# Block-sparse attention with a top-k expert: one-block steps of two batches rewritten as two-block units of one batch

## The chip, the cores and the metric

The kernel runs on one core of one Trainium2 chip. The metric is the device time of one execution in microseconds (us), taken as the median of several runs. The core has five engines with a program each: TensorE (PE) multiplies matrices into PSUM, VectorE (DVE), ScalarE (ACT) and GpSimd (POOL) work on tiles of 128 partitions, and SyncE (SP) issues DMA transfers. In the profile PEld is TensorE's weight load. GpSimd also issues DMA transfers whose rows are given by an index tile (gathers); they run on queue 0, SyncE's on queue 1, and both on the same 16 DMA engines.

## The reference

The inputs are q, k and v of 4 batches, 8 heads, 768 positions and 64 values per head, in float32. Positions fall into 24 blocks of 32. A query block sees the blocks beside it, itself, blocks 0 and 23, and three sampled blocks; query blocks 0 and 23 see everything.

```python
mask = np.abs(blk_i - blk_j) <= 1
mask = mask | (blk_i == 0) | (blk_j == 0) | (blk_i == 23) | (blk_j == 23)
for qb in range(24):
    for kb in sampled_blocks[qb]:
        mask[qb * 32:(qb + 1) * 32, kb * 32:(kb + 1) * 32] = True
attn = softmax(np.where(mask, q @ k.T / 8, -1e9))      # per batch and head
x = (attn @ v), heads side by side                      # [4, 768, 512]
scores = x @ w_gate                                     # [4, 768]
for b in range(4):                                      # the 128 best tokens of a batch
    top = argpartition(-scores[b], 128)[:128]
    ye = np.maximum(x[b, top] @ w1, 0) @ w2             # 512 -> 1024 -> 512
    out[b, top] = x[b, top] + sigmoid(scores[b, top])[:, None] * ye
```

## The kernel before

The work is a list of 60 tasks. 44 of them are interior tasks (`"i", h, i`): query block i (1 to 22) of the two batches 2h and 2h+1, all 16 heads. The other 16 are global tasks (`"g", b, c`): query blocks 0 and 23 of batch b against all 768 keys, for the two heads of pair c.

An interior task works as follows. `int_keys` lays eight key blocks for both batches side by side in a ring buffer `kg`: blocks 23, i-1, i, i+1 and the three sampled ones and block 0. VectorE copies the window of one batch, GpSimd that of the other (L295), and ScalarE the six sampled blocks, whose offsets it loads into registers. `int_values` loads the values of the window (`vw`, 96 rows of 4,160 bytes) over SyncE and gathers the sampled rows (`vr`) with GpSimd (L310). `int_scores` runs 32 matmuls of 64x32 weights over 256 key columns (L67 by way of `mm`), `int_softmax` takes the maxima and scales them, `int_exp` makes four exponentials, `int_transpose` turns the result in eight 128x128 pieces and evicts it on ScalarE and VectorE (which multiplies by `keep` to drop repeated blocks), and `int_out` runs 64 matmuls of 128x32 weights over 65 columns, normalises, stores the rows and adds up the gate's scores.

The tasks overlap by steps: in step s the scores of task s, the transposes of task s-1, the exponentials of task s and the output of task s-2 are issued. TensorE, VectorE, ScalarE and the loads keep the order in which they are written.

The routing (`route`) of a batch spreads the 768 scores over all partitions, builds comparison masks on VectorE (`p4`), counts them with matmuls on TensorE (`p5`), turns the ranks into a selection, and gathers the 128 chosen rows from the output. The expert splits every float32 operand into two float32r parts, so that a product is three. `expert(0, ...)` serves batches 0 and 1, `expert(2, ...)` batches 2 and 3; both run when the last attention tasks are ending or done, in an order written out by hand at the bottom of the function. In it, products with 256 and 512 columns alternate with the routing of batches 2 and 3.

Of the kernel before, what the change touches and what calls it, by code (L numbers as in the profile page):

```python
# [1 line left out]

# [15 lines left out]
PSUM = bass.MemoryType.PSUM  # L18

# [3 lines left out]
NPAIR = H // 2  # L23
VW = H * (D + 1)
# [4 lines left out]
NRING = 3  # L29
NKG = 3  # L30
WARM = 26
AHEAD = 1
SCALE = 0.125


@with_exitstack
def block_sparse_attention_moe(ctx, tc, qg, qi, kt, v1, blocks, w_gate, w1, w2, outs):
# [4 lines left out]
    inp = ctx.enter_context(tc.tile_pool(name="inp", bufs=3))  # L42
    ring = ctx.enter_context(tc.tile_pool(name="ring", bufs=1))
    work = ctx.enter_context(tc.tile_pool(name="work", bufs=3))
# [3 lines left out]
    ps_s = ctx.enter_context(tc.tile_pool(name="ps_s", bufs=2, space=PSUM))  # L48
# [4 lines left out]
    blk32 = blocks.bitcast(I32)  # L53
    flat = blk32.rearrange("(o a) b -> o (a b)", o=1)

    loads, pe, copied = [], [], []
    filled = set()
    inorder = [True]

    def queue(i):  # L60
        if inorder[0]:
            if pe:
                tc.add_manual_dep(i.ins, pe[-1].name, NOSYNC, reason="PE in order")
            pe.append(i.ins)

    def mm(*args, **kw):
        queue(nc.tensor.matmul(*args, **kw))  # L67

    def trans(*args, **kw):
        queue(nc.tensor.transpose(*args, **kw))  # L70


    class Pinned:
        """An engine whose instructions keep the order in which they are written."""

        def __init__(self, engine):
            self.engine, self.on, self.last = engine, True, None

        def __getattr__(self, name):
            def call(*args, **kw):  # L80
                i = getattr(self.engine, name)(*args, **kw)  # L81
                if self.on:
                    if self.last is not None:
                        tc.add_manual_dep(i.ins, self.last.name, NOSYNC, reason="in order")
                    self.last = i.ins
                return i
            return call

    vec, act = Pinned(nc.vector), Pinned(nc.scalar)

    def load(dst, src):
        i = nc.sync.dma_start(dst, src)  # L92
        if loads:
            tc.add_manual_dep(i.ins, loads[-1].name, NOSYNC, reason="loads in order")
        loads.append(i.ins)

# [1 line left out]
    def load_k(b, n):  # L98
        k_sb = ks[b] = inp.tile([P, NPAIR, NB, BLK], F32, tag="k", name=f"k{b}")
        c = NB // n  # L100
        return [lambda p=p, t=t: load(k_sb[:, p, t * c:(t + 1) * c], kt[b, :, p, t * c:(t + 1) * c])
                for p in range(NPAIR) for t in range(n)]

    def load_v(b):
        v_sb = vs[b] = inp.tile([P, S // P, VW], F32, tag="v", name=f"v{b}", bufs=1)
        src = v1[b // 2 * S:(b // 2 + 1) * S, (b % 2) * VW:(b % 2 + 1) * VW]
        if b == 0:
            c = 2 * (D + 1)
            return [lambda p=p: load(v_sb[:, :, p * c:(p + 1) * c],
                                     src[:, p * c:(p + 1) * c].rearrange("(t r) c -> r t c", r=P))  # L110
                    for p in range(NPAIR)]
        return [lambda t=t: load(v_sb[:, t], src[t * P:(t + 1) * P]) for t in range(S // P)]

    def load_qg(b):
        q_sb = inp.tile([P, NPAIR, P], F32, tag="qg", name=f"qg{b}", bufs=2)
        if b == 0:
            load(q_sb[:, 0], qg[b, :, 0])
            return q_sb
        load(q_sb, qg[b])
        return q_sb  # L120

    rb_i = const.tile([P, NB, 3, 2], I32, name="rb_i")
    qgs, qs, ks, vs = {}, {}, {}, {}
    qgs[0] = load_qg(0)
    lk, lv = load_k(0, 1), load_v(0)
    for t in range(2):
        load(ks[0][:, 0, 12 * t:12 * t + 12], kt[0, :, 0, 12 * t:12 * t + 12])
    load(rb_i.rearrange("p a b c -> p (a b c)"), flat.broadcast_to([P, NB * 6]))
    load(qgs[0][:, 1:], qg[0, :, 1:])
    lk[1]()  # L130
    for f in (lk[2], lv[0], lk[3], lv[1]):
        f()

# [4 lines left out]
    for t in range(WARM):  # L138
        nc.tensor.matmul(pw[:, 0:P], none, none, start=True, stop=True)
# [3 lines left out]
    nc.gpsimd.memset(ones, 1.0)  # L143
    warm = const.tile([P, 1], F32, name="warm")
    act.activation(warm, ones[:, 0:1], AF.Exp)
    upper = const.tile([P, P], F32, name="upper")
    nc.gpsimd.affine_select(upper, ones, pattern=[[1, P]], compare_op=ALU.is_gt, fill=0.0,
                            base=0, channel_multiplier=-1)
    one = const.tile([P, 1], BF16, name="one")
    vec.memset(one, 1.0)  # L150
    slot = const.tile([P, P], BF16, name="slot")
    nc.gpsimd.iota(slot, pattern=[[1, P]], base=0, channel_multiplier=0,
                   allow_small_or_imprecise_dtypes=True)
    # token of column c of the score row: blocks 0 and 23 come first
    tok = const.tile([P, S // P], F32, name="tok")
    nc.gpsimd.iota(tok, pattern=[[P, S // P]], base=-BLK, channel_multiplier=1,
                   allow_small_or_imprecise_dtypes=True)
    nc.gpsimd.iota(tok[0:BLK, 0:1], pattern=[[0, 1]], base=0, channel_multiplier=1,
                   allow_small_or_imprecise_dtypes=True)
    nc.gpsimd.iota(tok[BLK:2 * BLK, 0:1], pattern=[[0, 1]], base=S - BLK, channel_multiplier=1,  # L160
                   allow_small_or_imprecise_dtypes=True)

# [1 line left out]
    rb = const.tile([P, NB, 3], F32, name="rb")  # L164
    koff = const.tile([1, NB, 4], I32, name="koff")
    p32 = const.tile([P, 1], F32, name="p32")
    idx_f = const.tile([P, NB], F32, name="idx_f")
    idx = const.tile([P, 2, NB], U32, name="idx")
# [3 lines left out]
    dif = const.tile([P, NB, 3], F32, name="dif")  # L172
    keep = const.tile([P, NB], F32, name="keep")
    keep_w = const.tile([P, 1], F32, name="keep_w")
    d32 = const.tile([P, BLK], F32, name="d32")
    d64 = const.tile([P, 2 * BLK], F32, name="d64")
    tokb = const.tile([P, S // P, 2], BF16, name="tokb")

    # iden[p, q] summed over head quadrants: delta(p % 32, q) and delta(p % 64, q)
    vec.tensor_reduce(d32, ident.rearrange("p (h q) -> p q h", h=4), AX.X, ALU.add)  # L180
    vec.tensor_reduce(d64, ident.rearrange("p (h q) -> p q h", h=2), AX.X, ALU.add)
    # a token as two bf16 values that add to it
    vec.tensor_copy(tokb[:, :, 0], tok)
    vec.tensor_tensor(tokb[:, :, 1], tok, tokb[:, :, 0], ALU.subtract)
    # of the sampled blocks: their offsets in a row of keys, rows to gather
# [10 lines left out]
    for h in range(2):  # L196
        nc.gpsimd.tensor_scalar_add(idx[:, h], idx_f, float(h * S))
# [604 lines left out]
```

## Time and profile before

| | before |
|---|---|
| median of 3 runs | 362.99 us (362.63 to 365.73) |
| span of the profiled execution, first to last instruction | 362.1 us |
| busy: TensorE, VectorE, ScalarE, GpSimd | 282.0, 249.0, 198.9, 124.6 us |
| DMA | 71.20 MB, 197 GB/s over the span |

The page gives the profiled execution's span and no other time of it; the median of the runs is 0.9 us above that span. Times in the trace count from the start of the span. A row of a stretch (A:B) gives its length and then each engine's busy time with the number of its instructions, the granted TensorE clock as a share of full speed, the mean busy share of the DMA engines (which can exceed 1.0 by a little) and what they moved.

### The profile page before, as it was taken

The page shows a single profiled execution, that of the slowest core. Times are in us where ns is not written, and L with a number is a line of the kernel's source. Part 1 is how long each engine was busy: PE and PEld are TensorE (multiplying, and loading weights), DVE is VectorE, ACT ScalarE, POOL GpSimd, SP SyncE. Part 2 cuts the span into 40 slices and gives each one's busy share as a digit, 9 for nine tenths or more (in the row PEclk, how much of TensorE's full clock was granted, in tenths as well). Part 3 has the DMA queues.
Part 4 walks back from the last instruction along what each step waited for, and adds up shares of the span by engine and source line. Part 5 has one row for each costly group of instructions (what it writes and reads, how often), then busy time and mean ns, then how long its engine had stood idle before and what let it go on. Part 6 is the DMA issues. An engine that isn't in the chain of part 4 may idle for free.

```text
span 362.1 us, 14408 instructions
## 1 busy us (share of the span) xinstructions
PE 282.0 (78%) x5706; PEld 208.5 (58%) x5706; DVE 249.0 (69%) x792; ACT 198.9 (55%) x627; POOL 124.6 (34%) x192
## 2 busy tenths in 40 slices
PE   6972938395668978987667799775969999999992
PEld 4552725263446656664434576444657678878982
DVE  2772847656657997897499989987778976972010
ACT  2681729466747885485656468774657762321310
POOL 4850316444433421243453404322212312424421
PEclk9988776978986999999698999988789999999997
DMA  6999799988997997699999737799877510011000
GB/s 203 360 219 225 213 275 267 254 264 231 286 239 228 250 272 242 220 249 271 270 256 228 218 100 198 204 264 249 238 233 208 162 53 23 17 31 58 31 29 29
DMA packets 45162, 71.20 MB, mean 197 GB/s; under 512 B 6953, under 2 KB 29225, under 8 KB 45097
## 3 DMA queue, kind: packets, MB, share of 16 engines
q1 hardware_dynamic: 39529, 50.63, 50.8%
q0 software_dynamic: 5568, 19.67, 19.4%
q8 instruction: 45, 0.74, 0.9%
q14 instruction: 20, 0.16, 0.2%
HBM read 62.93 MB, written 7.35 MB: 194 GB/s over the span
## 4 chain that ended last, share of the span: by engine, by line
DMA 47%; PE 16%; DVE 14%; issue 9%; SPq 6%; POOL 3%; ACT 2%; POOLq 0%; ACTq 0%; DVEq 0%
DMA out<-x 11%; DMA vw<-v 11%; DMA v<-v 7%; DMA w<-w 7%; DMA q<-qi 5%; PE o L67 4%; SPq L92 4%; DVE c L81 3%; PE gs L67 3%; DVE mx L81 3%; PE pt L70 2%; SPq L379 2%; DMA k<-kt 2%; DMA sb<-row 2%; PE s L67 2%
## 5 line engine op out<-in xcount | busy, mean ns | idle before, releaser
L67 PE MATMUL o<-vw,tw 128*32 128x65 f32 x1408 | 51.4, 239 | 41.0 <-DMA vw<-v 27.6
L81 ACT ACTIVATE pr<-s,mx 128x256 f32<-128x256 f32 x176 | 69.2, 480 | 17.2 <-DVE mx L81 17.0
L310 POOL DMA_INDIRECT vr<-v,idx x44 | 42.6, 968 | 86.7 <-PE o L67 80.2
L67 PE MATMUL s<-kg,q 64*32 64x256 f32 x1408 | 57.8, 434 | 15.0 <-ACT kg L81 10.0
L67 PEld LDWEIGHTS o<-vw,tw 128*32 128x32 f32 x1408 | 38.1, 120 | 50.6 <-issue 48.3
L70 PE MATMUL pt<-ident,pr 128*128 128x128 f32 x352 | 61.3, 313 | 6.7 <-ACT kg L81 2.9
L70 PEld LDWEIGHTS pt<-ident,pr 128*128 128x128 f32 x352 | 44.7, 157 | 34.0 <-ACT pr L81 18.5
L81 DVE TENSOR_SCALAR tr<-pt,keep 128x256 f32<-128x256 f32 x88 | 40.0, 479 | 31.5 <-ACT tw L81 30.2
L81 ACT COPY kg<-k 128x128 f32 x264 | 57.5, 313 | 3.5 <-issue 2.9
L81 DVE TENSOR_REDUCE mx<-s 128x4 f32<-128x1024 f32 x44 | 53.5, 1217 | 2.2 <-PE s L67 2.1
L67 PE MATMUL o<-vr,tr 128*32 128x65 f32 x1408 | 51.2, 238 | 3.5 <-issue 3.5
L81 ACT COPY tw<-pt 128x256 f32<-128x256 f32 x84 | 30.5, 380 | 40.8 <-PE o L67 33.6
L295 POOL COPY kg<-k 128x384 f32<-128x384 f32 x44 | 23.3, 531 | 57.5 <-PE s L67 34.5
L67 PEld LDWEIGHTS o<-vr,tr 128*32 128x32 f32 x1408 | 39.6, 121 | 4.2 <-issue 4.1
L67 PEld LDWEIGHTS s<-kg,q 64*32 64x32 f32 x1408 | 23.9, 116 | 29.1 <-ACT kg L81 10.3
L81 DVE TENSOR_TENSOR x<-o,z 128x256 f32<-128x256 f32 x44 | 18.7, 424 | 20.1 <-DMA out<-x 18.4
L257 POOL TENSOR_TENSOR w_l<-w,w_h 128x512 fp32r<-128x512 f32 x16 | 21.3, 1333 | 24.6 <-ACT w_h L81 23.3
L81 DVE CUSTOM_DVE_ANT_0 j<-x,wg_i 128x128 f32<-128x128 f32 x88 | 26.3, 298 | 3.0
L67 PE MATMUL gs<-k,qg 128*128 128x384 f32 x64 | 25.7, 526 | 1.7 <-DMA k<-kt 1.7
L81 ACT CAST w_h<-w 128x512 fp32r<-128x512 f32 x16 | 10.0, 625 | 26.1 <-DMA w<-w 25.0
L81 DVE TENSOR_SCALAR c<-sb,sc 128x128 bf16<-128x128 f32 (+5 forms) x44 | 23.0, 562 | 0.1
L81 DVE COPY kg<-k 128x384 f32<-128x384 f32 (+1 forms) x68 | 22.4, 360 | 0.2 <-DMA k<-kt 0.2
(118 smaller groups left out, 396.2 us busy)
## 6 DMA issues: line engine op xcount, KB each, us to landing
vw<-v SPq DMA_DIRECT2D x44, 390.0 KB
q<-qi SPq DMA_DIRECT2D x44, 128.0 KB
out<-x SPq DMA_DIRECT2D x88, 64.0 KB
v<-v SPq DMA_DIRECT2D x18, 260.0 KB
k<-kt SPq DMA_DIRECT2D x11, 384.0 KB
w<-w SPq DMA_DIRECT2D x16, 256.0 KB
v<-v SPq DMA_DIRECT2D x4, 390.0 KB
k<-kt SPq DMA_DIRECT2D x12, 128.0 KB
```

What stands on the lines that cost most here:

```text
L67: queue(nc.tensor.matmul(*args, **kw))
L70: queue(nc.tensor.transpose(*args, **kw))
L81: i = getattr(self.engine, name)(*args, **kw)
L92: i = nc.sync.dma_start(dst, src)
L257: nc.gpsimd.tensor_tensor(wl, f, wh, ALU.subtract)
L295: copied.append(nc.gpsimd.tensor_copy(kgt[:, 1, :, 1:4], ks[2 * h + 1][:, :, i - 1:i + 2]).ins)
L310: nc.gpsimd.indirect_dma_start(out=vr[n][0:3 * BLK], out_offset=None, in_=v1[:, :], in_offset=bass.IndirectOffsetOnAxis(ap=idx[0:3 * BLK, ...
L379: nc.sync.dma_start(outs[b][i * BLK:(i + 1) * BLK].rearrange("q (p c) -> p q c", p=NPAIR), xe)
```

## The change

The kernel is written anew around the unit (`b, u`): the two query blocks 2u-1 and 2u of one batch, eight heads, 44 units in all. Four key blocks are shared by both query blocks (0, 23, 2u-1, 2u); each query block has four own ones besides: three sampled and the remaining neighbour. A repeated sampled block is replaced by the keys of another slot and an all-zero value row (a 25th block of zeros is added to the values), so no mask is multiplied.

- Shared keys are read in place by the score matmul; own keys are copied to `kr`, four sampled ones and the neighbours by GpSimd with offsets from registers (four loaded per unit), two sampled ones by ScalarE.
- Values of the own blocks are gathered by GpSimd (two gathers of 128 rows of 2,080 bytes per unit, into four buffers); those of the shared blocks are loaded by SyncE (64 rows per unit; blocks 0 and 23 once per buffer and batch, five buffers).
- Queries are scaled by 1/8 on VectorE before use, so maxima and exponentials need no scale.
- The global query blocks are two steps per batch, each for four heads.
- The 52 steps are laid out with fixed slots: in step s the transposes and output of step s, the exponentials of s+1, the scores and maxima of s+2 and the gather of s+3 are issued, and every engine, SyncE and GpSimd among them, keeps the written order.
- Weights are loaded and split in steps 1 to 18, the low part on VectorE (before: GpSimd).
- A batch's routing and expert are spread over 28 steps that begin after its last unit: ranks are counted on VectorE by comparisons that accumulate, and the expert runs on one batch with 512-column products. Batch 3 spreads its scores with a matmul instead of by way of DRAM.
- The area kept for GpSimd's DMA descriptors is set to 8,192 bytes per partition.

```diff
+    def load_vs(b, u):
+        i = vs_of(b, u)
+        r = rows_of(b, 2 * u - 1)
+        sp.dma_start(vss[i][0:64], vt[r:r + 64])
+        if vs_b[i] != b:
+            vs_b[i] = b
+            for n, j in enumerate((0, NB - 1)):
+                r = rows_of(b, j)
+                sp.dma_start(vss[i][64 + 32 * n:96 + 32 * n], vt[r:r + BLK])
...
+    def w_split(i):
+        if i in stage:
+            wh, wl, f = ws[i][0], ws[i][1], stage.pop(i)
+            act.copy(wh, f)
+            vec.tensor_tensor(wl, f, wh, ALU.subtract)
...
+    def gather(b, u):
+        kr = krs[b, u] = inp.tile([P, 2, NP, KW], F32, tag="kr", name=f"kr{b}_{u}", bufs=3)
+        vr = vrs[b, u] = inp.tile([P, 2, VR], F32, tag="vr", name=f"vr{b}_{u}", bufs=4)
+        for e in range(2):
+            pool.indirect_dma_start(
+                out=vr[:, e], out_offset=None, in_=vt[:, :],
+                in_offset=bass.IndirectOffsetOnAxis(ap=vidx[:, b, u - 1, e:e + 1], axis=0))
+        flat = ks[b].rearrange("p j c -> p (j c)")
+        o = offs.pop((b, u, POOL))
+        for e in range(2):
+            for s in range(2):
+                pool.tensor_copy(kr[:, e, s], flat[:, ds(o[2 * e + s], KW)])
+        w = [slot_of(2 * u - 2), slot_of(2 * u + 1) if u < NU - 1 else slot_of(0)]
+        pool.tensor_copy(kr[:, :, 3], ...)
...
+    def unit_scores(b, u):
+        t = [st.setdefault((b, u, g), ps_s.tile([P, 2, 8, BLK], F32, tag="s", name=f"s{b}_{u}_{g}")) for g in range(G)]
...
+                    pe.matmul(t[g][64 * p2:64 * p2 + 64, ph, 0:4], qs[b, u // 3][rows, u % 3, p],
+                              pairs(ks[b], rows, j, two, slice(p * BLK, (p + 1) * BLK)),
+                              start=ph == 0, stop=False, tile_position=(64 * g, 64 * p2), skip_group_check=True)
...
+                        pe.matmul(t[g][r0:r0 + 32, ph, 4:8], qs[b, u // 3][rows, u % 3, p, e],
+                                  krs[b, u][rows, e, :, p * BLK:(p + 1) * BLK],
+                                  start=False, stop=ph == 1, tile_position=(64 * g, r0), skip_group_check=True)
...
+    def maxima(t):
...
+            for g in range(G):
+                vec.tensor_reduce(mx[:, g], st[b, u, g].rearrange("p h k c -> p h (k c)"), AX.X, ALU.max, negate=True)
...
+        def rank(t):
+            sb, s, n = R["sb"], R["sc"][:, t:t + 1], t * P
+            junk = rout.tile([P, S], BF16, tag="cj", name=f"cj{b}_{t}")
+            if n:
+                vec.tensor_scalar(junk[:, :n], sb[:, :n], s, 0.0, ALU.is_ge, ALU.add, accum_out=R["rk"][:, t, 0:1])
+            vec.tensor_scalar(junk[:, n:], sb[:, n:], s, 0.0, ALU.is_gt, ALU.add, accum_out=R["rk"][:, t, 1:2])
+            vec.scalar_tensor_tensor(junk[:, n:n + P], sb[:, n:n + P], s, before, ALU.is_equal, ALU.mult,
+                                     accum_out=R["rk"][:, t, 2:3])
...
+        plan += [(4, "b", columns), (5, "a", columns_out)]
+        plan += [(5 + t, "c", lambda t=t: rank(t)) for t in range(6)]
+        plan += [(11, "a", select), (11, "b", chosen), (12, "a", fetch), (14, "b", xt), (15, "a", xt_out)]
+        plan += [(15 + i, "b", lambda i=i: w1_mm(0, 4 * i, 4 * i + 4)) for i in range(3)]
...
+        plan += [(23 + i, "b", lambda i=i: w2_mm(6 * i, 6 * i + 6)) for i in range(4)]
+        plan += [(27, "a", put)]
...
+    for s in range(n + 1):
...
+        if t3:
+            offsets(*t3)
+            gather(*t3)
+        run(s, "a")
...
+        if done:
+            norm(*done)
+        if s < n:
+            turn(steps[s])
+        if done:
+            gate(*done)
+        if s < n:
+            if s + 1 < n:
+                exps(steps[s + 1])
+            if t3:
+                gather_act(*t3)
...
+                unit_scores(*t2)
...
+                out_unit(*t)
+            run(s, "b")
...
+                maxima(steps[s + 2])
+            run(s, "c")
...
+    for s, where in sorted(due):
+        run(s, where)
```

## Rows read from the trace of the kernel before

**Rows 1.** The page: busy time of each engine (share, instructions); DMA busy tenths by slices.
```profile
PE 282.0 (78%) x5706; PEld 208.5 (58%) x5706; DVE 249.0 (69%) x792; ACT 198.9 (55%) x627; POOL 124.6 (34%) x192
...
DMA  6999799988997997699999737799877510011000
```

**Rows 2.** The page: chain of work that ended last, shares by engine.
```profile
DMA 47%; PE 16%; DVE 14%; issue 9%; SPq 6%; POOL 3%; ACT 2%; POOLq 0%; ACTq 0%; DVEq 0%
```

**Rows 3.** Stretches: length, busy time (instructions) of each engine, clock, DMA share, GB/s.
```profile
12.00:16.00 4.00, 4.00 (x50) 3.02 (x52) 3.33 (x10) 2.52 (x8) 3.26 (x12) 1.00 1.03 390
28.00:32.00 4.00, 0.59 (x6) 0.35 (x4) 1.63 (x3) 0.47 (x2) 0.31 (x1) 1.00 1.07 220
40.00:60.00 20.00, 12.95 (x346) 9.02 (x347) 11.75 (x37) 11.41 (x39) 7.18 (x8) 0.76 0.99 273
68.00:72.00 4.00, 0.00 (x0) 0.00 (x0) 2.73 (x8) 1.46 (x6) 1.35 (x2) 0.88 1.01 240
72.00:76.00 4.00, 3.54 (x96) 2.40 (x96) 2.02 (x6) 2.57 (x9) 1.20 (x2) 0.50 0.79 239
120.00:135.00 15.00, 12.61 (x352) 8.30 (x336) 14.05 (x48) 12.69 (x47) 4.74 (x6) 1.00 0.94 266
268.00:284.00 16.00, 14.30 (x395) 10.61 (x395) 12.99 (x49) 9.87 (x34) 3.58 (x5) 0.89 0.73 219
298.70:343.70 45.00, 43.94 (x415) 39.31 (x414) 24.17 (x76) 11.92 (x25) 17.21 (x20) 1.00 0.11 32
```

**Rows 4.** VectorE in order of time, one interior step: start us, us, instruction.
```profile
122.85 1.22 DVE L81 TENSOR_REDUCE mx<-s 128x4 f32<-128x1024 f32 x1
...
124.97 0.15 DVE L81 TENSOR_SCALAR z<-o 128x4 f32<-128x4 f32 x1
...
125.83 0.29 DVE L81 CUSTOM_DVE_ANT_0 j<-x,wg_i 128x128 f32<-128x128 f32 x1
...
126.65 1.22 DVE L81 TENSOR_REDUCE mx<-s 128x4 f32<-128x1024 f32 x1
```

**Rows 5.** DMA: all packets, and the queue of GpSimd's gathers (packets, MB, share).
```profile
DMA packets 45162, 71.20 MB, mean 197 GB/s; under 512 B 6953, under 2 KB 29225, under 8 KB 45097
...
q0 software_dynamic: 5568, 19.67, 19.4%
```

**Rows 6.** Groups by line and shape: busy us, mean ns of one, idle before, releaser.
```profile
L310 POOL DMA_INDIRECT vr<-v,idx x44 | 42.6, 968 | 86.7 <-PE o L67 80.2 <-PE selp L67 2.8 <-PE rp L67 2.1
...
L295 POOL COPY kg<-k 128x384 f32<-128x384 f32 x44 | 23.3, 531 | 57.5 <-PE s L67 34.5 <-DMA k<-kt 12.8 <-PE pt L70 10.2
...
L81 DVE TENSOR_REDUCE gmx<-gs 128x1 f32<-128x768 f32 x16 | 15.2, 952 | 3.8 <-PE gs L67 3.8
...
L81 DVE CUSTOM_DVE_ANT_0 gj<-xg,wg_g 128x256 f32<-128x256 f32 x4 | 1.8, 440 | 0.3 <-DVE xg L81 0.2
...
L81 DVE TENSOR_TENSOR x_hl<-xtp,x_hl 128x512 fp32r<-128x512 f32 x1 | 0.7, 692 | 4.5 <-ACT x_hl L81 4.5
```

**Rows 7.** VectorE in order of time, the masks of one rank piece.
```profile
310.75 0.62 DVE L81 TENSOR_SCALAR c<-sb,sc 128x768 bf16<-128x768 f32 x1
311.28 0.35 DVE L81 SCALAR_TENSOR_TENSOR d<-sb,sc,upper 128x128 bf16<-128x128 f32 x1
```

**Rows 8.** The chain in order of time: start us, us, work (TensorE at full clock).
```profile
275.04 1.04 PE o L67 x64
276.08 1.02 PE s L67 x32
277.11 1.02 PE pt L70 x8
...
323.12 1.49 PE yp L67 x6
```

**Rows 9.** Engines in order of time: the sampled blocks' arrival, and the last sum.
```profile
6.32 0.24 POOL L186 CAST rb<-rb_i 128x72 f32<-128x72 int32 x1 [4.27 <-DMA rb_i<-blocks]
...
355.19 0.48 DVE L81 SCALAR_TENSOR_TENSOR xe<-yp,ge,xe 128x256 f32<-128x256 f32 x1 [2.31 <-PE yp L67]
```

More of the change, by code (lines that the diff above doesn't have):

```diff
@@ L51, in block_sparse_attention_moe @@
     ps_m = ctx.enter_context(tc.tile_pool(name="ps_m", bufs=1, space=PSUM))
[L53 to L70, printed above, removed]
     class Pinned:
         def __init__(self, engine):
-            self.engine, self.on, self.last = engine, True, None
+            self.engine, self.last = engine, None
         def __getattr__(self, name):
@@ new lines, in block_sparse_attention_moe @@
+    pool.memset(own[rows, NU - 2, 1:2], float(NB))
+    key = const.tile([P, 1], F32, name="key")
+    for c in range(NP):
+        pool.iota(key[BLK * c:BLK * (c + 1)], pattern=[[0, 1]], base=0, channel_multiplier=1,
+                  allow_small_or_imprecise_dtypes=True)
+    vidx = const.tile([P, B, NU - 1, 2], I32, name="vidx")
+    vec.tensor_scalar(own, own, float(BLK), key, ALU.mult, ALU.add)
+    for b in range(B):
+        vec.tensor_scalar(vidx[:, b], own, float(b * VB * BLK), None, ALU.add)
@@ new lines, in pairs, with glob_scores @@
+    def pairs(k, rows, j, step, cols):
+        a = k[rows, j:j + 2, cols]
+        return bass.AP(a.tensor, a.offset, [a.ap[0], [step * KW, 2], a.ap[1], a.ap[2]])
+    def glob_scores(b, ph, h):
+        for g in range(G):
+            st[b, "g", ph, g, h] = ps_s.tile([P, 512], F32, tag="s", name=f"gs{b}_{ph}_{g}_{h}")
+        for p2 in range(2):
+            p = 2 * p2 + ph
+            for g in range(G):
+                rows = slice(64 * g, 64 * g + 64)
+                pe.matmul(st[b, "g", ph, g, h][64 * p2:64 * p2 + 64, 0:384], qs[b, 0][rows, 0, p],
+                          ks[b][rows, 12 * h:12 * h + 12, p * BLK:(p + 1) * BLK],
+                          start=True, stop=True, tile_position=(64 * g, 64 * p2))
@@ new lines, in norm, with gate, at, run @@
+                    sp.dma_start(outs[b][r0:r0 + BLK, c], x[64 * p2 + 32 * e:64 * p2 + 32 * e + 32])
+    def gate(b, u):
+        junk = work.tile([P, NP * D], F32, tag="junk", name=f"j{b}_{u}", bufs=1)
+        vec.tensor_tensor_reduce(junk, xs.pop((b, u)).rearrange("p h d -> p (h d)"), wg_i, 1.0, 0.0, ALU.mult, ALU.add,
+                                 sps[b][:, u:u + 1])
+    due = {}
+    def at(s, where, f):
+        due.setdefault((s, where), []).append(f)
+    def run(s, where):
+        for f in due.pop((s, where), []):
+            f()
@@ new lines, in xt_out, with w1_mm @@
+        def xt_out():
+            R["x"] = rout.tile([P, 2, 4, P], F32R, tag="x", name=f"x_hl{b}")
+            split(R["x"][:, 0], R["x"][:, 1], R["pm"])
+        def w1_mm(c, n0, n1):
+            if n0 == 0:
+                R["h1"] = mid(f"h1_{c}")
+            x = R["x"]
+            parts = [(x[:, i, t], w[:, t, c * 512:(c + 1) * 512])
+                     for i, w in ((0, w1_h), (0, w1_l), (1, w1_h)) for t in range(4)]
+            for n in range(n0, n1):
+                pe.matmul(R["h1"], *parts[n], start=n == 0, stop=n == 11)
```

973 lines of the change are left out of this document (393 added, 580 removed).

## Prediction

> **What bounds the kernel now.** I read the page's busy shares and slices first [rows 1], then the chain of waits [rows 2], then the stretches [rows 3]. No engine is full over the span: TensorE has 78%, VectorE 69%. The DMA engines, however, are at nine tenths or more in most slices up to 280 us and idle after it, and DMA has 47% of the chain. In [rows 3] the two regimes stand side by side. From 40 to 60 us the transfers move 273 GB/s at a share of 0.99, while TensorE works 12.95 of 20 us and VectorE 11.75: work waits for data. From 120 to 135 us VectorE is busy 14.05 of 15 us (94%), and a step of that stretch takes 3.8 us from one maximum to the next [rows 4]. So the attention part is bound by DMA where transfers pile up and by VectorE elsewhere. From 298.7 us on TensorE works 43.94 of 45 us at full clock: that is the expert of all four batches, run almost alone. Three parts are to be priced: start, steps, tail.
>
> **DMA.** Before, 71.20 MB move [rows 5]. Gathers: 44 units of 256 value rows of 2,080 B make 23.4 MB (queue 0 had 19.67 MB, 2.1 MB of it the chosen tokens in and out, which stay). Shared values: 64 rows for each of 44 units, and 64 more for each of 5 buffers in 4 batches, make 8.5 MB. The window's value loads (44 of 390 KB) and gathers made 17.6 + 17.6 MB, and the edge rows of the rings 1.6 MB; queries shrink by half a MB. Keys, whole-value tiles, weights, stores stay. The sum is 71.2 - 3.3 - 1.6 - 0.5 = 66 MB, 64 of it before the last unit. The rate: at full share 273 GB/s from 40 to 60 us, 390 GB/s from 12 to 16 us (key rows of 3 KB), 220 from 28 to 32 us, where 256-byte stores ran [rows 3]. The new transfers are rows of 1 to 3 KB to 64 or 128 partitions; I take 300, between, and keep 273 and 390. 64 MB then need 213 us (164 to 234). Batch 0, with the weights, two key sets and two whole-value tiles in its 13 steps, needs 19 MB, 63 us.
>
> **VectorE, the new bound.** Per unit: normalising 0.86 us (start of z to start of j [rows 4]); the 512-column eviction 0.69 (the one 128x512 subtraction from PSUM) and the gate over 256 columns 0.44 [rows 6]; two maxima of 512 columns. The reduction takes 1.22 us for 1,024 columns [rows 4] and 0.952 for 768 [rows 6], so 1.04 ns a column, and 0.67 each from start to start. That is 3.33 us against 3.8 now: the two copies into key rings, the scaling of maxima and one gate instruction go. Per batch: 11 units 36.7 us; two global steps with eight reductions of 384 columns (0.555 each by that slope), two evictions, one normalisation and gate, 7.4; four query scalings of 768 columns 2.4 (a comparison of 768 took 0.62 [rows 7]). That is 46.5.
> Ranks: the 24 mask pairs become 24 counts with accumulation. An accumulating instruction of VectorE grew from 0.29 us for 128 columns [rows 4] to 0.44 for 256 [rows 6], 1.1 ns a column; 768 columns then cost 0.8, with two starts, the third instruction (0.35 [rows 7]) and three reads of the accumulator 1.45 us. By the plain comparison (0.62 for all 768 columns) it would be 1.1; I take 1.45, as the new instruction accumulates. The Trainium skill (SBUF — State Buffer, Who interferes with whom) speaks against the edit too: it lets the plain `tensor_scalar` use two ports but not the form that writes an accumulator; no run here shows that form. Six ranks 8.7, selection and small pieces 2.3: 11 us. The expert's subtractions move in from GpSimd: three of 0.69 and the last sum 0.75, 2.8 us a batch. So do 16 weight subtractions, 9 us in batch 0 and 2 in batch 1. VectorE's work to the last unit is 55.5 + 59.5 + 60.3 + 59 = 234 us.
> It is not held at 100%. Before it had 94% from 120 to 135 us and 81% from 268 to 284 [rows 3]; between them I take 90%: 260 us for 52 steps, 5.0 each. The ends are 249 and 289. DMA (213, at most 234) lies under that; in batch 0 its 63 us sit beside 55.5/0.9 = 62, so it costs 1 at most.
>
> **What hides below it.** TensorE: at full clock 64 value products of 65 columns took 1.04 us, 32 score products of 256 columns 1.02, eight transposes 1.02 [rows 8]. Eight products on 64x64 tiles run four at once and sixteen on 64x32 tiles eight at once, all of 128 columns: 0.5 us, half. Values: eight two at once and sixteen four at once, 0.52, half. So 2.05 us a unit instead of 3.1; global scores fall to some 0.75 us a step. Rank counting leaves TensorE. The expert's 48 products of 512 columns cost 0.248 each (six in 1.49 us [rows 8]), 11.9 us a batch; the heaviest step holds six, 3.6 us in all. ScalarE (199 us busy before [rows 1]) loses four of six key copies a step and gains nothing as large. SyncE issues some 250 transfers as before.
> GpSimd: two gathers at 0.97 us [rows 6], four copies of 128 columns (0.53 for 384, so 0.24 each) and one of 256 (0.37): 3.3 us a unit against 1.5, plus four register loads, which no row shows on GpSimd. Below: nothing. Above: each like the small cast there, 0.24 us [rows 9], 1.0 together. I take 0.4, nearer the lower end, as the engine needs to compute nothing for them: 3.7 us, under 5.0. If that cover goes, the scores two steps on are late. The gather waits for the value product four units back, and the copies queue behind it.
>
> **Start and end.** The sampled blocks arrive at 6.3 us [rows 9]; 28 small VectorE instructions of some 0.2 us (z takes 0.15 [rows 4]) take 6 us, then GpSimd gathers three units of 3.3 us; the maxima of the second end at 21.5, where steps begin. Only the experts of batches 0 and 1 lie beside later batches; 2 and 3 follow the last unit. One expert is a chain: 11.9 us of products, 12 transposes 1.6, three splits and two rectifiers across ScalarE and VectorE with hand-overs, 5.5: 19 us. The second follows the first, as both use one PSUM tile; ranks of batch 3 hide beside batch 2's products except 2 us. Scores on chip 3, two chains 38, that 2, and from the last product to the end 0.95 + 6.4 (the last sum started at 355.19 [rows 9]; the span ends at 362.1), together 51 us, where 63 followed 298.7.
> Sum: 21.5 + 260 + 51 = 332.5 us of span. The profiled execution has no time beyond its span on the page; the runs' median is 0.9 us above it. Forecast: 333 us.
>
> **Rivals.** *GpSimd's gather sets the step (slower).* Place: gathers and dynamic copies of one unit in GpSimd's fixed order. Price: steps of 44 units at 6.2 us and 8 global ones at 4 give 305, 378 us in total. It decides from about 5.8 us a unit (363 in all). For: four offset loads, and a queue where each gather waits for a buffer. Against: 0.97 us a gather now, with GpSimd 34% busy [rows 1, 6]. Chance 0.16.
> *TensorE's clock falls.* With 2.05 of 5.0 us it is sparser than from 40 to 60 us, where 65% busy came with a granted clock of 0.76 [rows 3]. From 72 to 76 us it was 0.50, the 1.2 GHz level, behind four microseconds without a matmul; with 84% busy and short gaps it was 1.00, the 2.4 GHz level, from 120 to 135. At the lower level, steps with expert products take 5.5 to 6.4 us in batches 2 and 3, some 6 us a batch, and the tail's 27 us of matmul double: 333 + 12 + 27 = 372; at half the time 352. The Trainium skill (TensorE: Matmul & The Clock Gate, What's actually happening) calls the lower level the default that activity lifts; the rows agree. Gaps here are about 2 us, shorter than the one at 68 us. Chance 0.16, half of it above 366.
> *Little is lost between engines.* VectorE at 94%, transfers at 350 GB/s or more, ranks at 1.1 us: 333 - 11 - 8 = 314. Speaking for it: the fixed order is two units deep. Chance 0.13.
> *The gain is eaten.* VectorE's share stays at the 81% of 268 to 284 us: 21.5 + 289 + 51 = 362, no change. Chance 0.07.
>
> **How the numbers follow.** The forecast, 320 to 350, gets 0.48. Faster by over 1% (under 359.4; 1% is about what a measurement can tell): 0.48 + 0.13 + 0.07 of the clock case = 0.68. Within 1%: 0.07 and 0.02 of the clock case. Slower: 0.16 + 0.07 = 0.23. The range takes in both unknown prices above and leaves out the worst of the gather and the best of the third case: 308 to 371.
>
> **What would show it.** Right: VectorE near 90% busy from 22 to 280 us; queue 0 near 25.5 MB and about 66 MB in all; a unit's value products about 0.5 us and its scores 0.5; steps of 5.0 us; the last unit near 281 us; a tail of 51 us in which TensorE shows gaps of about 1.5 us at each split. Wrong: GpSimd over 5.5 us a unit with scores waiting for its copies; a granted clock near 0.5 in the tail; a DMA share of 0.95 past batch 0; a start after 25 us; rank counts near 1.1 us.

## The result, and the profile after

The changed kernel takes 349.61 us (median of 4 runs, 346.28 to 350.06) against 363.31 us for the kernel before on the same chip (4 runs, 362.63 to 365.73): a ratio of 0.9598, 95% interval 0.9532 to 0.9664. It is 4% faster where 8.3% was forecast. (Ratios and intervals leave out the runs in the chip's slower state, so a ratio here need not be the quotient of two medians.) The profiled execution took 350.02 us with a span of 348.2, which is 15.7 us over the 332.5 of the sum.

The page of the kernel after: busy time and instructions of each engine, chain of waits by engine, all DMA packets, and the queue of GpSimd's gathers.
```profile
PE 276.8 (79%) x5508; PEld 206.0 (59%) x5508; DVE 234.7 (67%) x697; ACT 155.6 (45%) x400; POOL 165.9 (48%) x356
...
DMA packets 32038, 65.78 MB, mean 189 GB/s; under 512 B 5736, under 2 KB 12136, under 8 KB 31976
...
q0 software_dynamic: 7680, 25.53, 24.4%
...
PE 44%; DVE 20%; issue 15%; DMA 11%; ACT 5%; POOL 2%; SPq 1%; POOLq 1%; ACTq 0%; DVEq 0%
```
Against [rows 1, 2, 5]: the 66 MB and the 25.5 MB are as forecast, and DMA's share of the chain falls from 47% to 11%. But TensorE, meant to lose a third of its work in each unit, is at 276.8 us where it had 282.0, and it now has the largest part of the chain.

Stretches of the kernel after (length, busy time with instructions of TensorE, its weight loads, VectorE, ScalarE, GpSimd; clock, DMA share, GB/s). First four stretches of about a batch each, then the end, then single steps from one normalisation to the next: one with a weight subtraction, one with nothing but a unit, one with a rank, one with a rank and four products of the expert's first layer.
```profile
20.00:85.00 65.00, 50.55 (x1256) 37.61 (x1248) 45.29 (x111) 37.25 (x96) 40.77 (x84) 0.98 0.91 285
85.00:153.00 68.00, 55.23 (x1362) 41.68 (x1363) 58.55 (x172) 37.86 (x100) 39.65 (x83) 0.95 0.80 245
153.00:220.00 67.00, 61.02 (x1358) 45.58 (x1357) 53.65 (x162) 35.75 (x95) 39.38 (x84) 1.00 0.76 231
220.00:288.00 68.00, 61.69 (x1275) 46.14 (x1274) 50.30 (x158) 33.12 (x85) 30.57 (x63) 1.00 0.49 137
288.00:348.20 60.20, 41.09 (x148) 29.54 (x147) 19.26 (x64) 7.02 (x13) 5.01 (x9) 0.80 0.07 22
...
56.30:59.80 3.50, 3.37 (x109) 2.65 (x104) 3.43 (x10) 2.84 (x9) 0.96 (x1) 1.00 0.69 184
...
153.00:156.50 3.50, 3.50 (x108) 2.79 (x107) 3.15 (x11) 2.44 (x7) 2.88 (x6) 1.00 0.89 234
129.80:134.30 4.50, 3.50 (x104) 2.77 (x104) 4.40 (x17) 2.40 (x8) 3.22 (x8) 1.00 0.89 277
...
195.70:200.20 4.50, 4.50 (x110) 3.49 (x108) 4.40 (x17) 2.96 (x9) 3.68 (x8) 1.00 0.87 268
```
The maxima of the second unit, the forecast's mark for the start of the steps, end at 21.5 us, as forecast (start us, us, instructions, idle time before):
```profile
20.28 1.29 DVE L67 TENSOR_REDUCE mx<-s 128x2 f32<-128x512 f32 x2 [2.43 <-PE s L67]
```
The steps run from there to the last normalisation at 287.9 us: 266.4 us where 260 was forecast. The end is 60.3 where 51 was. Look at the four single steps. With a weight subtraction TensorE has 3.37 and VectorE 3.43 of 3.50 us. With a unit alone TensorE is full and VectorE is not (3.15). With a rank VectorE alone is full. In the last step both are. Over the four batches TensorE is busy 228.5 of 268 us (85%), VectorE 207.8 (78%).

The chain of waits of the kernel after, interior steps of batch 2 (start us, us, work).
```profile
195.03 0.87 PE pt L67 x8
195.90 1.20 PE s L67 x48
197.09 1.21 PE o L67 x48
198.31 1.14 PE h L67 x4
199.45 0.87 PE pt L67 x8
```
It stays on TensorE through whole steps. Scores take 1.20 us and values 1.21, where 0.5 and 0.52 were forecast and where two blocks took 1.02 and 1.04 before [rows 8].

### The profile page after: what moved, and what is told of

It is laid out like the page before. It is cut to its first block, busy times and chain, and to the rows that moved or that the text cites. A ratio compares the mean times of both kernels' runs of the same rounds, so it can differ in the third digit from the quotient of the medians.

```text
span 348.2 us, 13754 instructions
## 1 busy us (share of the span) xinstructions
PE 276.8 (79%) x5508; PEld 206.0 (59%) x5508; DVE 234.7 (67%) x697; ACT 155.6 (45%) x400; POOL 165.9 (48%) x356
## 4 chain that ended last, share of the span: by engine, by line
PE 44%; DVE 20%; issue 15%; DMA 11%; ACT 5%; POOL 2%; SPq 1%; POOLq 1%; ACTq 0%; DVEq 0%
PE o L67 11%; PE s L67 9%; PE pt L67 7%; PE h L67 5%; DVE mx L67 5%; DMA w<-w 5%; PE y L67 4%; PE gs L67 4%; DVE cj L67 3%; DVE gm L67 3%; ACT pr L67 3%; PE go L67 3%; DMA k<-kt 2%; DVE w_l L67 1%; DVE pc L67 1%
## 5 line engine op out<-in xcount | busy, mean ns | idle before, releaser
L67 POOL DMA_INDIRECT vr<-vt,vidx x88 | 88.0, 1001 | 74.3 <-PE o L67 28.3
L67 DVE TENSOR_REDUCE mx<-s 128x2 f32<-128x512 f32 x88 | 56.5, 682 | 23.7 <-PE s L67 22.2
L67 POOL COPY kr<-k 128x128 f32 (+1 forms) x220 | 63.1, 330 | 4.9 <-PE s L67 4.6
L67 ACT COPY pc<-pt 128x512 f32<-128x512 f32 x44 | 25.7, 585 | 64.5 <-PE pt L67 64.5
L67 PE MATMUL o<-vs,pc 128*64 128x65 f32 x704 | 30.9, 229 | 18.4 <-ACT pr L67 8.6
L67 PE MATMUL s<-k,q 64*64 64x128 f32 x704 | 31.8, 296 | 9.4 <-DMA vs<-vt 8.1
L67 PE MATMUL s<-kr,q 64*32 64x128 f32 x1408 | 32.0, 286 | 7.0 <-POOL kr L67 3.6
L67 PE MATMUL o<-vr,pc 128*32 128x65 f32 x1408 | 31.0, 225 | 3.3 <-issue 3.3
L67 DVE COPY pc<-pt 128x512 f32<-128x512 f32 x44 | 30.0, 683 | 3.1 <-PE pt L67 2.7
L67 DVE TENSOR_SCALAR_CACHE_REDUCE cj<-sb,sc 128x128 bf16<-128x128 f32 (+5 forms) x44 | 26.7, 641 | 0.1
```

## The experiments

Runs that were measured together on one chip are called a session. Medians below are compared with the kernel before, which ran in every session, or with the changed kernel where that ran too. "Batch ends" are the last normalisations of the batches in the profiled execution; in the kernel after they are 87.9, 153.0, 220.1 and 287.9 us.

The first theory, A: TensorE sets the steps, and its gaps and clock set the end. Its rival: VectorE and its ranks set the steps.

**e1**: `pe.matmul(fill, none, busy)` with zeros, three to five products of 512 columns in each gap of the tail.

> The changed kernel with idle products (512 columns of bf16 zeros into a spare PSUM tile) put on TensorE into the gaps of the tail, three before each transposition of the rectified half and five behind each group that a split follows; nothing else differs. Theory A (the tail is 9 us longer than forecast because the granted clock falls to 0.5 to 0.9 in the gaps of 0.7 to 1.5 us that the splits leave): the products of 512 columns return to 0.23 us each, the tail shortens by 6 to 10 us, time 340 to 344. Rival (the tail is long because of the chain of splits and ranks themselves): no change within 2 us, or some us slower as the fillers stand in the way, 348 to 353.

347.11 us against 365.21 (ratio 0.9437, 0.9338 to 0.9536). The tail was 52.8 us, the mean clock in it 0.96 where the kernel after has 0.80. That speaks for A's second half (gaps and clock set the end), but no run of the unedited changed kernel was made beside it.

**e2**: the shared value products of one head pair instead of four.
```diff
-        for i in range(NP):
-            for p2 in range(2):
-                h = p2 * 4 + i
+        for p2 in range(2):
+            h = p2 * 4          # i = 0 alone
```


> The changed kernel without 6 of the 8 products per unit of the shared value rows (their contribution is left out), which takes 12 of 48 value instructions, some 0.5 us of TensorE, from each of 44 units; all else as it is. Theory A (TensorE is what bounds the steps without ranks, as its work per unit is 3.4 us and not the 2.05 forecast): a plain step falls from 3.4 to 3.0 us and steps with expert products by 0.4 to 0.5; with the rank steps unmoved the time falls by 10 to 16 us, to 334 to 340. Rival (VectorE bounds the steps, as forecast): at most 4 us, 346 to 350.

346.12 us (0.9431, 0.9337 to 0.9526); batch ends 85.0, 150.6, 217.0, 284.8. Batches 1 to 3 keep their length (65.6, 66.4 and 67.8 us; 65.1, 67.1 and 67.8 in the kernel after): A is not borne out. The cut was smaller than meant, though: the shared value products take 0.32 us a unit where they took 0.62, so 0.3 us left TensorE and not 0.5.

**e3**: no rank counts; a fixed list of tokens goes to the expert.
```diff
-        plan += [(5 + t, "c", lambda t=t: rank(t)) for t in range(6)]
```


> The changed kernel without the rank counts on VectorE (18 instructions a batch and their accumulator reads, 1.5 us in each of 24 steps; fixed ranks stand in, so other tokens go through the expert). Theory A (TensorE and VectorE take turns as the bound; VectorE only in the six rank steps of a batch, which take 4.5 us where TensorE needs 3.4): batch 1 gains some 6 us, batches 2 and 3 less as expert products run in the same steps, the tail 1 or 2: 8 to 14 us, time 336 to 342. Rival (VectorE is the bound throughout, as forecast): 18 steps of 1.5 us, 24 to 28 us, time 322 to 326.

343.56 us (0.9429, 0.9331 to 0.9528); batch ends 90.8, 153.3, 220.6, 287.1. Some 6 us for 34 us of VectorE's work (busy 201.0 us instead of 234.7): the rival falls too, as a bound of the whole.

**e4**: a weight piece every second step instead of every step (`if s % 2`).

> The changed kernel with one weight piece loaded and split every second step (steps 1 to 35) instead of every step (1 to 18). Theory A (batch 0 is bound by DMA, 19 MB in 65 us, and the weight pieces wait 10 and 6 us in the chain): 2 MB move from batch 0 to batches 1 and 2, where DMA has room, and the time falls by 6 to 10 us, to 340 to 344. Rival (the waits only move to the next load in the queue, or the subtractions on VectorE, now beside the ranks, cost as much there): within 3 us, 347 to 352.

346.71 us (0.953, 0.9447 to 0.9613). Batch 0 ended at 80.6 instead of 87.9, and more than half of that was gone by the last batch (284.9).

**e5** (e2 and e3 together), **e6** (the 1.3 MB load of a batch's values as six loads in six steps) and **e7** went to one chip, without the changed kernel itself. e7 reorders the tail: the products of a half-layer stand in the other half's evictions, with banks of their own:
```diff
+            if b >= 2:
+                return ps_s.tile([P, 512], F32, tag="s", name=f"{name}{b}")
...
+            plan += [..., (z + 1, "b", lambda: w1_mm(0, 0, 12)), (z + 2, "a", lambda: relu(0)),
+                     (z + 2, "b", lambda: w1_mm(1, 0, 12)), (z + 3, "a", lambda: relu(1)), (z + 3, "b", lambda: ht(0)), ...]
```


> Both cuts of the two earlier runs at once: 6 of 8 products of the shared values per unit left out, and no rank counts on VectorE (fixed ranks stand in). Each alone took some 6 us. Theory A (TensorE at 3.4 us and VectorE at 3.3 to 4.8 us a step are matched, so that taking from one leaves the other): together clearly more than the sum of 12, 16 to 24 us below the changed kernel, 326 to 334. Rival (what holds the steps is neither, but waits for transfers and the chain of the global steps): about the sum or less, 337 to 344.

> The changed kernel with the whole-value tile of the next batch (1.3 MB) loaded in six pieces over steps 8 to 12 of a batch instead of at once in step 9 (batch 0's own over steps 1 to 3). Theory A (behind this load SyncE's queue stands 7 to 9 us in three batches and TensorE's own instructions and the weight pieces come late; the chain shows 10 us there in batch 0, 3 in batch 1): time falls 6 to 12 us, to 338 to 344, and no gap of over 2 us by 'issue' is left on TensorE. Rival (the same bytes in the same stretch, DMA being full there): within 3 us, 347 to 352.

> The changed kernel with the experts of batches 2 and 3 reordered, the work the same: each product group has a PSUM tile of its own, both halves of the first layer run back to back, the second layer in two halves behind one wait, and batch 3's ranks start three steps earlier. Theory A (the tail of 60 us is two chains in which TensorE waits for each split and runs at a fallen clock): two of four waits a chain go and the clock stays up, tail 46 to 50 us, time 336 to 341. Rival (the tail is held by the rank counts of batch 3 and the gathers between): tail above 55 us, time 344 or more.

e5 351.71 us (0.9592, 0.953 to 0.9655), e6 366.06 (0.9997, 0.9951 to 1.0043), e7 356.55 (0.9749, 0.9687 to 0.9811). In e7 the tail fell to 47.8 us, but batches 2 and 3 took 73.0 and 71.8 us although the edit touches nothing before their end. A run in which e4, e6, e7 and fillers were put together (**e8**) took 358.62 (351.54 to 359.63), far from the 324 to 332 hoped for. Without a control none of this could be read: was it the edits or the place? The next session asked that (theory C), tested A once more, and put e4 and e7 together (**e11**) and with fillers (**e12**).

> The changed kernel itself, beside e10 to e12 and the kernel before, so that all four share a chip. Theory C (the long batches of e5 to e8, 69 to 75 us for batches 1 to 3 where the first four profiles had 65 to 68, come from the chip and not from the edits): here the changed kernel also shows either all its batches at 65 to 68 us or all at 69 to 75, whatever the edits beside it show, and its ratio to the kernel before is 0.96 to 0.985 on a chip with long batches, 0.955 to 0.965 on one with short ones. Rival (the edits made the batches long): 65 to 68 us here, ratio 0.96, and 69 to 75 in e11 and e12, which keep the tail of e7.

**e10**:
```diff
-                    r0 = 64 * p2 + 32 * e
-                    pe.matmul(o[r0:r0 + 32, i], mine[:, i, r0:r0 + 32], vr[:, e, ...], ...)
+                r0 = 64 * p2
+                pe.matmul(o[r0:r0 + 64, i], mine[:, i, r0:r0 + 64], vr[:, i % 2, ...], ...)   # scores likewise
```


> The products with a unit's own keys and own values are made for both blocks at once from the first or the second block's gathered keys (16 score products instead of 24 and 16 value products instead of 24 in a unit), so half of the sampled blocks are the wrong ones. TensorE issues 32 instructions fewer of the 96 to 104 in each of 44 units, some 0.8 us of its 3.4 at 25 ns each. Everything else is issued as before. Theory A (TensorE's instructions set the step): 20 to 35 us faster than e9_changed_again, batches 1 to 3 at 58 to 62 us. Rival B (the chain of evictions, maxima and exponentials between TensorE, VectorE and ScalarE sets it): under 8 us faster, since none of that chain changes.

> The last two experts' steps put so that a group of TensorE work of one batch stands in the other's evictions, with banks of their own (as e7), and the weight pieces loaded every second step (as e4); the 1.3 MB value load in one piece. If the tail's term is made of TensorE's gaps and low clock: 10 to 16 us faster than e9_changed_again (tail 46 to 50 us, batch 0 2 to 7 us shorter). If the gains of e4 and e7 are given back elsewhere (batches 2 and 3 longer by the tail's order): under 4 us faster.

> e11 with products of zeros on TensorE in the gaps that are left in the tail. If the granted clock is what is left of the tail's excess: tail 42 to 46 us, 2 to 5 us faster than e11. If the reordering has already closed the gaps: within 2 us of e11.

e9 349.85 us (345.07 to 352.49), e10 344.50 (341.05 to 346.08), e11 338.06 (335.42 to 341.05), e12 335.77 (332.21 to 336.63); before 364.84. e12 is 0.9185 of the kernel before (0.9094 to 0.9277), 14.1 us under the changed kernel's median beside it (e9) and 9.3 under its lowest run.

e10's 5 us look like rival B, but the page shows that the edit did not do what it was made for. The groups of own products, first of e9:
```profile
L67 PE MATMUL s<-kr,q 64*32 64x128 f32 x1408 | 31.8, 287 | 8.4 <-issue 4.2 <-POOL kr L67 4.1
L67 PE MATMUL o<-vr,pc 128*32 128x65 f32 x1408 | 31.7, 227 | 4.5 <-issue 4.5
```
and of e10 (busy us, mean ns of one, idle before):
```profile
L67 PE MATMUL s<-kr,q 64*64 64x128 f32 x704 | 29.0, 282 | 5.3 <-POOL kr L67 5.3
L67 PE MATMUL o<-vr,pc 128*64 128x65 f32 x704 | 30.4, 231 | 0.0
```
Half the instructions on tiles twice as wide take the same time. So e10 said nothing on A, and its 5 us may come from the stops told of in the last section, of which it has fewer.

The tails of e12 and of the kernel after differ in TensorE's clock; e12's from its last unit to the end:
```profile
287.10:333.40 46.30, 38.05 (x180) 27.37 (x180) 19.37 (x65) 6.81 (x13) 5.00 (x9) 0.98 0.09 30
```
46.3 us at 0.98, where e9's took 55.3 at 0.91; e11, without fillers, took 47.4 at 0.89. The order of the work gives some 8 us of it at nearly the same clock, the fillers 1 in the tail; the weights, spread as in e4, bring batch 0's end from 86.6 (e9) to 83.3.

**e13 to e16**, on one chip, with theory D, formed from e3 and e10: TensorE and VectorE take turns. e13 was made to take time from TensorE for certain:
```diff
+        for g in range(G):
+            pe.matmul(t[g][:, :, 4:8], none, zeros, ...)        # bfloat16 zeros
...  4 of 16 own score products, 4 of 16 own value products stay
```


> Leaves out 12 of the 16 score products and 12 of the 16 value products with a unit's own keys; two bfloat16 products of zeros fill the scores' columns instead, so TensorE's time for a unit falls by about 1.0 us of its 3.4 (44 units), all other engines do what they did. Theory A (TensorE sets every step): 35 to 44 us faster than e16_control. Theory D (TensorE sets the steps without a rank or an expert's split, VectorE sets those with them, through the single bank of the value products that the norm must read first): 12 to 28 us faster, the rank steps as long as before (4.4 to 6.5 us), the plain ones 1 us shorter. Rival B (the chain between engines sets all): under 8 us.

> e13 with the rank counts left out as well (a fixed list of rows goes to the expert). Theory D: 12 us or more faster than e13, against the 6 us that leaving out the ranks gave with TensorE as it was, since now neither engine covers the other. Theory A: about as e13, 5 to 7 us faster for the tail's and first rank's share alone. Rival B: under 14 us faster than e16_control in all.

e15 is e12 with `norm(*done)` ahead of `prefetch(s)` and `run(s, "a")`.

> e12 with one change: VectorE's norm of the unit before stands ahead of the scaling of q and of the experts' splits in its queue, so the bank of the value products is read first. Theory D says the wait of the value products in steps with a split or a scaling (about 1.4 us each, some 8 steps a batch) shrinks: 4 to 15 us faster than e12's 0.9185 of the kernel before, ratio 0.88 to 0.91. If VectorE then waits for the value products with the splits behind it, no change or up to 5 us slower: ratio 0.915 to 0.93.

> The changed kernel itself, on the chip of e13 to e15: 347 to 353 us, ratio 0.95 to 0.965 to the kernel before, batches 1 to 3 at 65 to 69 us. On a chip like that of e5 to e8: 354 to 358, batches at 69 to 75.

e13 350.06 us (0.9578, 0.952 to 0.9637), e14 332.67 (0.9129, 0.9055 to 0.9204), e15 353.69 (0.9688, 0.9621 to 0.9756), e16 367.07 (1.005, 1.0011 to 1.0089). The control is 17 us slower than in two other sessions (349.85 in e9 and again in e17), at the same time of the kernel before. So what made e5 to e8 look long need not be an edit: e16's batches 1 to 3 take 69.8, 73.6 and 73.0 us with none. Theory C is right that the kernel's time depends on the session. It is wrong about the chip: e1 to e4 ran at 343 to 347 us on the chip that gave e16.

The traces tell the two kinds of session apart. TensorE's waits for nothing ahead of the score loads (last section) come to 18 to 24 us in the kernel after, e1 to e4, e9, e11, e12 and e17, and to 39 to 41 in e5 to e8, e15 and e16. So e3 may be set beside the kernel after, and e16, though from another session, is the nearest control for e5 to e7 (the kernel before took 366.41 us beside them and 365.09 beside e16): e5 is 15.4 us under it, e6 1.0, e7 10.5. Cutting the load (e6) gained nothing, reordering the tail (e7) did, and e5, both cuts at once, gained more than e2 and e3 together (3.5 and 6).

e13, like e10, did not do what it was made for. Its own products, and the zeros in their place:
```profile
L67 PE MATMUL s<-kr,q 64*32 64x128 f32 x352 | 19.7, 296 | 3.5 <-POOL kr L67 3.2 <-issue 0.3
L67 PE MATMUL s<-zeros,none 128*128 128x256 bf16 x88 | 18.3, 292 | 0.3 <-issue 0.3
L67 PE MATMUL o<-vr,pc 128*32 128x65 f32 x352 | 15.0, 239 | 1.1 <-issue 1.0
```
Beside e9's 31.8 and 31.7 us that is some 10 us less in 44 units, 0.2 to 0.3 us a unit and not 1.0: the zeros cost more than the scores saved. Its 17.0 us under the control prove nothing either, as e13 at 350.06 us stands where the changed kernel stands in the other kind of session. The step with a weight subtraction takes 3.50 us as before, and not 1 us less.

Between e13 and e14 the session and TensorE's work are the same, and there leaving out the ranks is worth 17.4 us, against some 6 in e3. What it is worth in a step can be read from five rows (columns as above). In batch 1, in a step without products of the expert, e3 and then e13:
```profile
129.90:133.40 3.50, 3.50 (x106) 2.80 (x106) 3.04 (x10) 2.44 (x7) 2.96 (x7) 1.00 0.56 130
...
129.70:134.10 4.40, 3.24 (x58) 2.29 (x58) 4.30 (x15) 2.42 (x8) 3.25 (x8) 1.00 1.01 305
```
In batch 2, in the step with four products, e3, e13 and e14:
```profile
195.20:199.60 4.40, 4.40 (x109) 3.48 (x110) 3.10 (x9) 2.44 (x7) 3.52 (x7) 1.00 0.92 227
...
197.90:202.30 4.40, 4.40 (x74) 3.26 (x77) 4.29 (x17) 3.13 (x10) 3.70 (x8) 1.00 0.91 263
...
189.30:193.40 4.10, 4.10 (x64) 2.96 (x63) 3.06 (x9) 2.44 (x7) 3.48 (x8) 1.00 0.87 251
```
The kernel after has 4.50 us in both places. Without products the step loses 1.0 us with its rank (e3; the step before it 1.3) and is then full of TensorE's work; with the rank left in and TensorE relieved a little (e13) it stays at 4.4, full of VectorE's. With products, leaving out the rank alone buys 0.1 us, because TensorE is full as well, and relieving TensorE alone buys 0.1; both together buy 0.4 here, though nothing in the step before (4.3 to 4.4 us in all four kernels). So with ranks it is as D says: each engine covers the other. Why this comes to 17.4 us in e14 and 6 in e3 is not shown in full; part of e3's gain went into stops of TensorE, one of 2.74 us in batch 1. e15's gain over its control (13.4 us, 3.6%) is no more than e12's over e9 (14.1, 4.0%): moving the norm brought nothing that shows, and the part of D on splits and the wait of the value bank stays an argument, not a finding.

**e17, e18**: control and e10's kernel once more.

> The kernel of e10 (own products of both blocks in one, half of the sampled blocks the wrong ones; 1,408 products fewer, TensorE's time as before). If the supply of TensorE's instructions makes the difference between chips: 341 to 348 us whatever the control does, so 12 us or more under a control of 360 or more, 5 under one of 350. If something else does: 5 us under the control on either, so 355 or more beside a slow control.

349.85 and 344.52 us: the same 5 us as before, and the control did not come out slow, so the question that e18 was for is still open.

## Why the prediction came out at half the gain

Direction, transfers, the start of 21.5 us and VectorE's new instructions were right; the steps' 260 us and the end's 51 were too short by 6.4 and 9.3, which make the 15.7 us. Two steps of the prediction failed: TensorE's time for a unit, and the clock of the end, which the sum put at nothing.

**The first step that failed: "Eight products on 64x64 tiles run four at once and sixteen on 64x32 tiles eight at once ... 0.5 us, half. ... So 2.05 us a unit instead of 3.1."** TensorE takes 1.20 + 1.21 + 0.87 to 1.02 = 3.3 to 3.4 us a unit, more than before. The count went wrong: the 64 and 32 of [rows 8] are instructions in the trace, for which the code before has 32 and 16 calls; the 24 and 24 products of the new unit are calls in the code. The page after, like e9's lines above, lists 704 and 1,408 instructions where 44 units with 8 and 16 calls make 352 and 704: every float32 product is two instructions. So 64 and 32 had to be set against 48 and 48. Doubled, the forecast's own terms are 1.0 and 1.04 us; the other 0.2 us of each is not explained by any run. What the text said of tiles was right: e10 shows that two 32-wide products cost what one 64-wide does.

**From it followed "VectorE, the new bound" at 90%.** VectorE had been priced too high, and the price was only partly made good by ranks of 1.54 us instead of 1.45 (below). A unit alone was forecast at 3.33 us and takes 2.97 from one normalisation to the next:
```profile
150.02 0.14 DVE L67 TENSOR_SCALAR z<-o 128x4 f32<-128x4 f32 x1
...
150.41 0.42 DVE L67 TENSOR_TENSOR x<-o,z 128x256 f32<-128x256 f32 x1
150.75 0.68 DVE L67 COPY pc<-pt 128x512 f32<-128x512 f32 x1
...
152.99 0.15 DVE L67 TENSOR_SCALAR z<-o 128x4 f32<-128x4 f32 x1
```
The sum added up whole durations, but an instruction can start before the one ahead has ended (the second line ends at 150.83, the third starts at 150.75). Over 44 units that is 16 of the 26 us by which VectorE's 207.8 us from 20 to 288 us fall short of the 234 of the sum. And VectorE was held less well, 78% of the time and not 90%. The two errors nearly cancel, so that 260 us came within 6.4 is luck. TensorE, with 3.3 to 3.4 us, or 4.5 with four products of the expert, sets the steps with a unit alone and those with products, VectorE those with a rank; where a step has both, the two are equal. That is why e2 and e3, on one engine each, gave little.

The counts with accumulation, in order of time on VectorE (start us, us), and a whole rank from its first count to the next normalisation:
```profile
119.60 1.00 DVE L67 TENSOR_SCALAR_CACHE_REDUCE cj<-sb,sc 128x768 bf16<-128x768 f32 x1
...
132.75 0.60 DVE L67 TENSOR_SCALAR_CACHE_REDUCE cj<-sb,sc 128x384 bf16<-128x384 f32 x1
...
134.29 0.15 DVE L67 TENSOR_SCALAR z<-o 128x4 f32<-128x4 f32 x1
```
768 columns take 1.00 us, the plain comparison 0.62 [rows 7]. The choice of the dearer price was right. The Trainium skill (SBUF — State Buffer, Who interferes with whom) keeps the form that writes an accumulator out of the two-port modes; the 1.00 is in line with that.

**The second step that failed: "One expert is a chain ... 19 us", which assumed full clock.** From the first split to the last sum they took 23 and 25 us. TensorE in order of time in the kernel after (the bracket is idle time before and what ended it):
```profile
318.34 2.08 PE L67 MATMUL h<-w_h,x_hl 128*128 128x512 f32 x4 [1.46 <-DVE x_hl L67]
320.21 1.91 PE L67 MATMUL h<-w_l,x_hl 128*128 128x512 f32 x4
321.92 1.91 PE L67 MATMUL h<-w_h,x_hl 128*128 128x512 f32 x4
```
and its clock in stretches:
```profile
292.00:296.00 4.00, 2.60 (x14) 2.01 (x13) 0.69 (x1) 1.02 (x2) 1.11 (x2) 1.00 0.17 66
...
320.00:324.00 4.00, 3.83 (x9) 2.46 (x8) 0.00 (x0) 0.08 (x1) 0.00 (x0) 0.50 0.00 0
```
At 0.50, the 1.2 GHz level, behind a gap of 1.46 us at the split, the twelve products take from 318.34 to 323.83, some 5.5 us; at 1.00 the same twelve took 3.06 (the chain from 293.96). The gaps of about 1.5 us at the splits were forecast; the price put on them in the rival "TensorE's clock falls" (27 us, full doubling) was too high, in the sum (nothing) too low: the level fell in part of the end only, 0.80 over its 60.2 us. It is not the same in every execution: in the same order e9's tail ran at 0.91 and took 55.3 us, and e1's, with zeros in the gaps, at 0.96 and took 52.8. So 5 to 7.5 of the 9.3 us go with the clock, and the rest is hand-overs and what the zeros cost. The Trainium skill (TensorE: Matmul & The Clock Gate, What's actually happening) has the lower level as the default that activity lifts: e12's 0.98, with zeros multiplied in the gaps, agrees.

**The other rivals.** GpSimd's gather: a unit takes 2 x 1.00 for the gathers, 4 x 0.31 and 0.40 for the copies, 3.6 us where 3.7 was forecast, and sets none of the steps shown. DMA: batch 0 was costed at 1 us at most. It ends at 87.9 us, and the chain of waits stands on one weight piece for ten of them:
```profile
72.62 10.03 DMA w<-w
```
With the weights spread (e4) the batch ends at 80.6 us, so DMA cost more there, though e4 takes some of the subtractions out of the batch too. What it cost over the whole run can't be told, as later batches took much of it back.

## What to carry to other kernels

Count work in the same unit on both sides: instructions of the trace against instructions of the trace, not against calls in the code. When a change lightens one engine, price the step on every engine before naming the bound: here a rank's 1.5 us, taken from VectorE, shortened a step by 1.0 to 1.3 us where TensorE had room and by 0.1 where it was full. Before adding up durations, look whether the instructions overlap; before reading the time of a run that leaves something out, look at its own lines (e10 and e13 took far less from TensorE than was meant). And a drain at the end of a kernel, a chain of product, eviction, product, should have its groups interleaved: here the order alone was worth some 8 us of 55.

## What the hardware showed that was not expected

**TensorE can stop in the middle of a group with nothing to wait for.** Weight loads in order of time, first a unit's scores in e9 (the bracket is idle time before it):
```profile
158.18 0.42 PEld L67 LDWEIGHTS s<-k,q 64*64 64x64 f32 x16 [0.17 <-issue]
158.78 0.40 PEld L67 LDWEIGHTS s<-kr,q 64*32 64x32 f32 x32 [0.17 <-issue]
```
and in e16, the same kernel in another session:
```profile
162.86 0.42 PEld L67 LDWEIGHTS s<-k,q 64*64 64x64 f32 x16 [0.17 <-issue]
163.46 0.53 PEld L67 LDWEIGHTS s<-kr,q 64*32 64x32 f32 x25 [0.17 <-issue]
164.61 0.10 PEld L67 LDWEIGHTS s<-kr,q 64*32 64x32 f32 x1 [0.61 <-issue]
165.33 0.14 PEld L67 LDWEIGHTS s<-kr,q 64*32 64x32 f32 x2 [0.62 <-issue]
166.22 0.17 PEld L67 LDWEIGHTS s<-kr,q 64*32 64x32 f32 x4 [0.74 <-issue]
```
The 32 loads are broken up by three stops of 0.6 to 0.7 us. Over the run such waits are, in e9:
```profile
PEld s L67 <- issue: 21.8, 82, 3.6
```
and in e16 (us in total, times, longest):
```profile
PEld s L67 <- issue: 40.4, 117, 2.6
```
The 18.6 us between them are nearly the 20.5 us between the spans (346.2 and 366.7). The same lines are at 19.4 and 18.7 us in e13 and e14, which ran beside e16 with 3,484 matmul instructions instead of 5,508, and at 6.2 in e10, with 4,100 and none of its own products 32 wide. Over all of TensorE's weight loads, though, such waits are 62.9 us in e16, 44.3 in e9, 58.6 in e13, 55.6 in e14 and 22.8 in e10: in e13 and e14 they were not gone but stood ahead of values and zeros. A DMA queue for instructions, q8, moved 0.70 MB in 43 packets in both e9 and e16, 0.52 in e10 and 0.46 in e13, so its bytes follow TensorE's instructions. A supply that falls behind where the instructions are shortest would fit e10 and hardly e13. It stays an argument: no run varied the supply by itself, and nothing here shows what differs between the sessions.

**One large load holds the queue of loads.** SyncE of the kernel after (start us, us), behind the 1.3 MB load of the next batch's values:
```profile
73.24 7.02 SPq L67 DMA_DIRECT2D vs<-vt  x3
```
Three small loads take 7.02 us to issue, where three take 1.93 us at 82.22. TensorE stands 2.78 us in the middle of a score group in that time (at 80.43, "issue"). With the load cut in six (e6) no such group of small loads takes over 2.92 us to issue, so it is the large load that holds the queue. Nothing was gained by it: e6 is only 1.0 us under e16, its nearest control.
